# Attention and mixture-of-experts on one core: each pair's load of queries and keys issued four steps earlier on ScalarE's queue

## The chip, the cores and the metric

The kernel runs on one core of one Trainium2 chip. The metric is the device time of one execution in microseconds (us). Engines are named as in the profile: PE (TensorE), PEld (its weight loads), DVE (VectorE), ACT (ScalarE), POOL (GpSimd), SP (SyncE). A q behind a name (ACTq, SPq) is that engine's sequencer, which also issues its DMAs: an issue does not occupy the arithmetic of the engine, but it stands in the engine's program order, and a wait in front of it holds back whatever follows on that engine.

## The reference, cut to what matters

The input holds 8 batches of 8 heads with 576 positions and a head width of 64. Attention is thresholded: per query only the keys whose score is within tau of the row's maximum are kept. Its result, 4608 tokens of width 512, goes through a mixture of 8 experts, one expert per token.

```python
scores = scale * np.matmul(q, k.transpose(0, 1, 3, 2))
thresh = np.max(scores, axis=-1, keepdims=True) - tau
scores = np.where(scores >= thresh, scores, -1000000000.0)
attn = softmax(scores)
x = (attn @ v) as tokens [4608, 512]
expert_idx = argmax(x @ w_gate)
out[token] = gate * relu(x @ w1[expert]) @ w2[expert]
```

## The kernel before, in words

**Pairs and steps.** Two heads form a pair, so there are 32 pairs (n = 0 to 31), four to a batch. The order of the instructions of every engine is written out by hand: a loop (`one_step`, L1333) counts a step number k, each pair takes 10 steps, and what is planned for step k is issued in four slots of it (FRONT, BET, MID, END). Pair n's second set of scores, the exponentials, the masks and the casts stand in steps 10n to 10n+9; its first set of scores (for the maxima) stands 20 steps earlier. In the first, attention, part of the profile a step takes some 1.5 us (a pair took 14.84 us from 63.52 to 78.36 us).

**What a pair needs before its scores.** Every product is made in split precision, so queries and keys are brought in as 32-bit numbers and turned into a high and a low 16-bit part:

- `load_qk(n)`, L287: one DMA of 576 KB from HBM into a tile `qkf`; there are two `qkf` buffers, so the load of pair n writes over that of pair n-2. For n above 2 it is issued by ACT. Its step is given below.
- `split(n)`: an activation in place on ACT (L301, it scales), four steps later a cast to the high part on ACT (L303), one step after that the low part on POOL (L304). L304 is the last reader of `qkf`.
- `stack(n)` at step 10n-30: six copies on SP's queue (L319, L320, L321, after a small constant fill, L314) out of the tile `z` into the operands QK and ck, and two on ACT's queue into CQ (L325, three steps apart at the most).
- `row(p)`, L433: three DMAs of 2.2 KB on ACT's queue that put the row maxima of pair n (tile ptT) into CQ. The last of them stands three or four steps ahead of the pair's second scores, which read it.

```python
k = NSTEP * (n - 1) - LEAD - SL
if n >= 2:
    plan(max(first, k - LL), lambda n=n: load_qk(n))
if n > 1:
    plan(max(first + 1, k - TUNE["sp0"]) if n > 2 else first + 1, lambda n=n: split(n))
if n:
    plan(max(first + 3, k) if n > 1 else first + 2, lambda n=n: stack(n))
```

Here NSTEP, LEAD and SL are all 10, sp0 is 8 and first is -20. So k is 10n-30, the split stands at 10n-38, and the load at 10n-30-LL.

**The batch's transposing transfers.** When the last pair of a batch (n = 3, 7, 11, ...) has left PSUM, `finish(b)` plans for each of its four or five token blocks a transposing DMA on SP's queue (L629). For batches 0 to 5 they stand at steps 10n+37 to 10n+39, two to a step. With m = n+8 this is 10m-43 to 10m-41: they share their first step with the load of pair m as long as LL is 13. So six loads (m = 11, 15, 19, 23, 27, 31) stand beside such transfers.

**The rest.** SP also issues the load of the values (L291) and, later, those of the experts' weights. After attention the experts' products (h and y, L377) fill PE to the end.

Of the kernel before, what the change touches and what calls it, by code (L numbers as in the profile page):

```python
# [45 lines left out]
CAP = NTOK  # L46

TUNE = dict(
    lgp=6, rkp=6, hi=4, lo=5, rd=5, lead=10, r0=2, rs=1, r2=1, pl=0, pa=3, q0=1, qd=1, lgs=2, rks=2, c1=2, c3=1, c5=1, sl=10, ll=13, sp0=8, sps=0, lv=-9, sv=5, t0=16, av=2, tr=4, d=2, lg=5, d5=2, d6=2, d7=1, lg7=15, km=16, rate=15, dh=1, do=3, w1d=5, plv=1, xv=3, so=0, sto=0, ord=0, sc=5, fa=3, fd=4, wa1=-70, w2=38, wa2=-86, wl1=-28, wl2=-6, avb=2, route=1, ranks=7, pp=8, ew=4, maskat=0, w1a=-35, w0=19, w1b=3,
)  # L50


# [1409 lines left out]
```

## Time and profile before

| | us |
|---|---|
| median of 3 runs | 923.08 |
| lowest and highest run | 919.82, 925.15 |
| profiled execution, its own time | 923.2 |
| its span (first to last instruction) | 921.4 |
| PE busy | 887.7 (96% of the span) |
| DVE busy | 646.7 (70%) |
| ACT busy | 612.4 (66%) |
| POOL busy | 566.0 (61%) |

Shares are of the whole span and mix two stages: attention, up to about 490 us, where four engines work side by side, and the experts, where PE works nearly alone. A wait matters where PE idles; the view of waits by engine tells how often and for whom. DMA queues are named by number in the profile (q1 is that of SP, q10 that of ACT).

### The profile page before, as it was taken

Reading aid. Unit: us, or ns where it says so; the run is one execution under the profiler, and the core shown is the slowest. Engines: PE = TensorE matmul, PEld = TensorE weight load, DVE = VectorE, ACT = ScalarE, POOL = GpSimd, SP = SyncE. Lnnn points to the kernel's source line nnn. Section 1 sums busy time; section 2 is a strip of 40 time slices with the busy share of each in tenths; the row PEclk is TensorE's granted clock in tenths of the full one; section 3 lists DMA queues with packets and bytes.
Section 4 is the critical chain, followed back from the end, with each engine's and each line's share of the span. In section 5 each row is a group of like instructions: output and inputs, shape, how many; then the busy total and the mean of one; then the engine's idle time right before and its main releaser. Section 6 shows DMA issues by size and latency. Waiting matters only on the chain.

```text
span 921.4 us, 25091 instructions
## 1 busy us (share of the span) xinstructions
PE 887.7 (96%) x9983; PEld 643.0 (70%) x9983; DVE 646.7 (70%) x1322; ACT 612.4 (66%) x1040; POOL 566.0 (61%) x483
## 2 busy tenths in 40 slices
PE   4899999999999999999998999999999999999996
PEld 1377777777777677777776858666666666667773
DVE  7999898989898889898998856745333341524551
ACT  4789999999989889999889534444333351533561
POOL 7579887999999989989989733323222222222122
PEclk8999999999999999999999999999999999999998
DMA  8555484585774865956747695999565765547540
GB/s 200 136 124 132 111 172 119 154 188 137 194 164 133 155 143 164 190 138 175 142 130 147 215 191 193 292 306 344 165 201 159 178 174 164 180 147 225 183 173 27
DMA packets 173908, 158.14 MB, mean 172 GB/s; under 512 B 130201, under 2 KB 146075, under 8 KB 173788
## 3 DMA queue, kind: packets, MB, share of 16 engines
q1 hardware_dynamic: 152956, 105.38, 46.5%
q0 software_dynamic: 8992, 29.18, 9.5%
q10 hardware_dynamic: 11840, 21.94, 8.7%
q8 instruction: 80, 1.31, 0.6%
q14 instruction: 40, 0.33, 0.1%
HBM read 90.56 MB, written 19.17 MB: 119 GB/s over the span
## 4 chain that ended last, share of the span: by engine, by line
PE 78%; issue 6%; POOL 5%; DVE 4%; DMA 3%; ACT 2%; SPq 0%; ACTq 0%; POOLq 0%
PE h L377 19%; PE y L377 17%; PE st L447 7%; PE s L392 6%; PE s L396 6%; PE st L377 6%; PE av L536 4%; PE av L517 4%; PE av L542 3%; PE av L546 2%; PE av L547 2%; PE av L545 2%; POOL pl L484 2%; DVE nm L408 1%; DMA out_dram<-o,gt 1%
## 5 line engine op out<-in xcount | busy, mean ns | idle before, releaser
L484 POOL TENSOR_TENSOR pl<-e,ph 128x1024 f16<-128x1024 f32 x95 | 204.0, 2147 | 41.5 <-ACT ph L483 36.3
L408 DVE TENSOR_REDUCE nm<-s 128x1 f32<-128x512 f32 (+1 forms) x320 | 202.2, 637 | 14.7 <-PE s L396 9.9
L377 PE MATMUL y<-wb,hl 128*128 128x512 f16 (+2 forms) x1104 | 196.8, 347 | 1.7 <-issue 1.7
L377 PEld LDWEIGHTS <-wb 128*128 128x128 f16 x2304 | 183.1, 98 | 20.7 <-issue 2.8
L377 PE MATMUL h<-xTm,wb 128*128 128x256 f16 (+3 forms) x2112 | 190.1, 251 | 2.1 <-issue 2.1
L948 DVE SCALAR_TENSOR_TENSOR wb<-wf,wb 128x1024 f16<-128x1024 f32 x96 | 118.5, 1267 | 71.6 <-ACT wb L945 70.2
L377 PEld LDWEIGHTS <-hl 128*128 128x128 f16 (+2 forms) x1104 | 89.0, 98 | 100.0 <-issue 4.3
L392 PE MATMUL s<-QK 128*128 128x512 f16 (+3 forms) x640 | 138.0, 293 | 11.1 <-POOL QK L137 8.1
L1094 POOL DMA_INDIRECT out_dram<-o,gt x39 | 45.2, 1159 | 160.3 <-ACT o L1091 151.7
L396 PE MATMUL s<-ck,CQ 128*128 128x512 f16 (+3 forms) x640 | 142.5, 291 | 0.0
L447 PE MATMUL st<-QK 128*128 128x512 f16 (+3 forms) x640 | 135.7, 289 | 4.8 <-DVE e L478 2.9
L478 DVE SCALAR_TENSOR_TENSOR e<-st,e 128x512 f32<-128x512 f32 x192 | 129.5, 676 | 13.5 <-ACT e L475 11.9
L475 ACT ACTIVATE e<-st,ntau 128x512 f32<-128x512 f32 x192 | 131.0, 685 | 7.3 <-PE st L377 4.7
L945 ACT ACTIVATE wb<-wf 128x1024 f16<-128x1024 f32 x96 | 98.2, 1052 | 52.9 <-DMA wf<-in_w_dram 39.8
L377 PE MATMUL st<-CQ,ck 128*128 128x512 f16 (+3 forms) x640 | 130.7, 286 | 1.0 <-DMA CQ<-ptT 1.0
L459 ACT ACTIVATE e<-st,ntau_f 128x512 f32<-128x512 f32 (+1 forms) x160 | 93.6, 610 | 23.4 <-PE st L377 19.8
L517 PEld LDWEIGHTS av<-vf,e 128*128 128x128 f32 x512 | 91.6, 190 | 20.0
L483 ACT CAST ph<-e 128x1024 f16<-128x1024 f32 x96 | 99.6, 1037 | 5.9 <-issue 3.6
L1042 ACT ACTIVATE hl<-h 128x512 f16<-128x512 f32 (+2 forms) x78 | 43.9, 572 | 86.3 <-PE h L377 78.5
L546 PE MATMUL av<-vop,pl 128*128 128x65 f16 x768 | 96.5, 194 | 1.1 <-POOL pl L484 1.1
L545 PE MATMUL av<-vop,ph 128*128 128x64 f16 x768 | 96.6, 193 | 0.0
L547 PE MATMUL av<-vop,ph 128*128 128x65 f16 x768 | 95.6, 193 | 0.0
(227 smaller groups left out, 1547.6 us busy)
## 6 DMA issues: line engine op xcount, KB each, us to landing
wf<-in_w_dram SPq DMA_DIRECT2D x96, 512.0 KB
QK<-z SPq DMA_DIRECT2D x124, 144.0 KB
qkf<-in_qk_dram ACTq DMA_DIRECT2D x29, 576.0 KB
vf<-in_v_dram SPq DMA_DIRECT2D x31, 320.0 KB
ck<-z SPq DMA_DIRECT2D x62, 72.0 KB
CQ<-z ACTq DMA_DIRECT2D x58, 72.0 KB
x<-in_qk_dram SPq DMA_DIRECT2D x6, 288.0 KB
CQ<-ptT ACTq DMA_DIRECT2D x96, 2.2 KB
```

Source lines behind the costliest of these rows:

```text
L377: x = nc.tensor.matmul(*a, **kw).ins
L392: nc.tensor.matmul(sc[rows, oc], d["QA"][a][:, cols], d["KB"][a][:, CH[c]], start=True, stop=False)
L396: nc.tensor.matmul(sc[rows, oc], d["CQ"][:, at:at + cols.stop - cols.start], d["CK"][a][:, CH[c]], start=False, stop=True,)
L408: nc.vector.tensor_reduce(o, sc[:, 0:width(t)], axis=AX.X, op=ALU.max, negate=True)
L447: nc.tensor.matmul(sc[rows, oc], d["KB"][a][:, cols], d["QA"][a][:, CH[c]], start=True, stop=False)
L475: nc.scalar.activation(pf, sc, AF.Exp, bias=ntau, scale=0.125 / SS)
L478: masks.append(nc.vector.scalar_tensor_tensor(pf, sc, 0.0, pf, ALU.is_ge, ALU.mult).ins)
L484: (nc.vector if (n, t) in PLV else nc.gpsimd).tensor_tensor(l, pd, h, ALU.subtract)
L517: nc.tensor.matmul(av[:, a], d["Pf"][tv][:, q], vf[:, tv], start=False, stop=False)
L545: nc.tensor.matmul(av[rows, a, 0:D], h, vop[:, tv, W:W + D], start=False, stop=False)
L546: nc.tensor.matmul(av[rows, a], l, vop[:, tv, 0:W], start=False, stop=False)
L948: low = nc.vector.scalar_tensor_tensor(o[:, :, 1], x, SW, o[:, :, 0], ALU.mult, ALU.subtract)
```

## The change

One number of the table that sets the order is another: LL, by which the load stands ahead of `stack(n)`, is 17 in place of 13.

```diff
 TUNE = dict(
-    ..., sl=10, ll=13, sp0=8, ...
+    ..., sl=10, ll=17, sp0=8, ...
 )
```

The load of pair n moves from step 10n-43 to step 10n-47. Their number, size and source are the same. The load of pair 2, on SP's queue, keeps its place, since the earliest step bounds it; that of pair 3 moves past no other instruction and that of pair 4 past one cast; the 27 others, of pairs 5 to 31, move past some 13 rows of ACT each. Nothing is moved on PE, DVE, POOL and SP through the whole of attention.

ACT around the load of pair 23, before, at the place where the load will stand. L301 is the split of pair 22, L325 the second query copy of pair 21, L433 a row of maxima of pair 19, and L475 and L459 are exponentials of pair 18:

```order
L475 ACTIVATE e_2_5925<-st_2_5922,ntau 128x512
L425 ACTIVATE ptT_5920<-pst_5918,thr 9x128
L301 ACTIVATE qkf_5817<-qkf_5817 128x1152
L475 ACTIVATE e_2_5925<-st_3_5952,ntau 128x512
L325 DMA CQ_105<-z_5629 64x576
L459 ACTIVATE e_8_5982<-st_8_5977,ntau_f 128x512
L459 ACTIVATE e_10_5989<-st_10_5984,ntau_f 128x64
L427 CAST ptT_5920<-pst_5918 9x128
L433 DMA CQ_107<-ptT_5920 1x9x128
```

The same place of ACT in the changed kernel:

```order
L301 ACTIVATE qkf_5658<-qkf_5658 128x1152
L475 ACTIVATE e_2_5925<-st_3_5952,ntau 128x512
L325 DMA CQ_105<-z_5629 64x576
L287 DMA qkf_5962<-in_qk_dram 128x1152
L459 ACTIVATE e_8_5984<-st_8_5979,ntau_f 128x512
L459 ACTIVATE e_10_5991<-st_10_5986,ntau_f 128x64
L427 CAST ptT_5920<-pst_5918 9x128
L433 DMA CQ_107<-ptT_5920 1x9x128
L483 CAST ph_0_5878<-e_0_5877 128x1024
```

The load of pair 23 now stands between the query copy and the exponential L459, and ahead of all three rows of maxima (L433). Before, it stood behind the three rows:

```order
L475 ACTIVATE e_4_6079<-st_4_6076,ntau 128x512
L433 DMA CQ_107<-ptT_5920 1x9x128
L303 CAST z_5934<-qkf_5817 128x2x576
L475 ACTIVATE e_4_6079<-st_5_6104,ntau 128x512
L287 DMA qkf_6114<-in_qk_dram 128x1152
L598 CAST R_194<-xn_5872 128x4x128
```

The row L287 is gone from this place; the others stand there as before.

SP in the same steps reads alike in both kernels (here of the change): the last three copies of pair 21, a load of values, the five transposing transfers of batch 3, and then pair 22:

```order
L319 DMA QK_1_8416<-z_8154 64x2x576
L320 DMA QK_1_8416<-z_8154 64x1152
L321 DMA ck_1_99<-z_8154 64x576
L291 DMA vf_111<-in_v_dram 128x10x64
L629 DMA_TRANSPOSE xTg_0_8641<-R_195 128x8x128 x2
L629 DMA_TRANSPOSE xTg_2_8664<-R_195 128x8x128 x2
L629 DMA_TRANSPOSE xTg_4_8686<-Rh_196 128x8x128
L314 DMA CQ_106<-before 3x18x64
L319 DMA QK_0_8717<-z_8459 64x2x576
```

By program step the load stood beside the transposing transfers; it now stands beside the copies of pair 21, ahead of the transfers.

## Rows read from the trace of the kernel before

**Rows 1.** The page: the span, and PE's busy time.

```profile
span 921.4 us, 25091 instructions
PE 887.7 (96%) x9983; PEld 643.0 (70%) x9983; DVE 646.7 (70%) x1322; ACT 612.4 (66%) x1040; POOL 566.0 (61%) x483
```

**Rows 2.** Busy by stretch: PE, PEld, DVE, ACT, POOL, then clock, DMA share, GB/s.

```profile
50.00:485.00 435.00, 432.98 (x5834) 330.43 (x5833) 394.96 (x851) 392.67 (x719) 395.75 (x258) 1.00 0.65 151
```

**Rows 3.** Waits of PE, whole execution: total us, times, longest us.

```profile
PE st L447 <- DVE e L478: 2.9, 5, 1.5
...
PE s L392 <- DMA ck<-z: 1.6, 1, 1.6
```

**Rows 4.** Waits of all engines from 300 to 326 us.

```profile
DVE e L478 <- ACT e L475: 2.7, 2, 2.5
ACT qkf L301 <- DMA qkf<-in_qk_dram: 2.7, 1, 2.7
...
PE st L447 <- DVE e L478: 1.5, 1, 1.5
```

**Rows 5.** ACT in order of time, 300 to 326 us: start, us, line.

```profile
303.35 0.52 ACTq L325 DMA_DIRECT2D CQ<-z  x1
...
305.22 0.69 ACT L459 ACTIVATE e<-st,ntau_f 128x512 f32<-128x512 f32 x1 [0.30 <-PE st L377]
...
310.30 0.33 ACTq L287 DMA_DIRECT2D qkf<-in_qk_dram  x1
...
320.45 1.16 ACT L301 ACTIVATE qkf<-qkf 128x1152 f32<-128x1152 f32 x1 [2.73 <-DMA qkf<-in_qk_dram]
```

**Rows 6.** SP's queue in order of time, at two batches' transposing transfers.

```profile
122.62 9.57 SPq L629 DMA_TRANSPOSE xTg<-R  x4
...
308.19 12.00 SPq L629 DMA_TRANSPOSE xTg<-R  x4
```

**Rows 7.** As rows 2: around the load of pair 23, and around that of pair 8.

```profile
304.00:308.00 4.00, 4.00 (x86) 3.32 (x83) 3.99 (x11) 3.45 (x7) 3.98 (x4) 1.00 0.74 219
...
310.00:312.00 2.00, 2.00 (x21) 1.66 (x21) 1.57 (x3) 2.00 (x4) 2.00 (x2) 1.00 1.12 192
312.00:314.00 2.00, 2.00 (x25) 1.47 (x24) 1.92 (x4) 1.87 (x4) 1.84 (x3) 1.00 1.78 94
314.00:316.00 2.00, 2.00 (x19) 1.35 (x18) 1.99 (x5) 2.00 (x6) 2.00 (x2) 1.00 0.48 34
...
86.00:88.00 2.00, 2.00 (x21) 1.75 (x20) 1.92 (x4) 1.86 (x4) 2.00 (x2) 1.00 0.66 259
```

**Rows 8.** ACT in order of time, a pair without transposing transfers (load of pair 8).

```profile
76.52 0.54 ACTq L325 DMA_DIRECT2D CQ<-z  x1
78.10 0.69 ACT L459 ACTIVATE e<-st,ntau_f 128x512 f32<-128x512 f32 x1 [0.43 <-PE st L377]
...
83.48 0.72 ACTq L433 DMA_DIRECT2D CQ<-ptT  x1
84.30 0.42 ACTq L287 DMA_DIRECT2D qkf<-in_qk_dram  x1
...
90.80 1.15 ACT L301 ACTIVATE qkf<-qkf 128x1152 f32<-128x1152 f32 x1
```

**Rows 9.** The tile qkf, whole execution: engines' idle time that a load ended.

```profile
  DMA qkf<-in_qk_dram: 2.7, 1
```

**Rows 10.** SP and PE in order of time: pair 6's last copy, pair 4's and 6's first scores.

```profile
76.64 0.60 SPq L321 DMA_DIRECT2D ck<-z  x1
...
86.93 0.38 PE L447 MATMUL st<-QK 128*128 128x512 f16 x1
...
87.52 0.38 PE L392 MATMUL s<-QK 128*128 128x512 f16 x1
```

**Rows 11.** POOL and ACT in order of time, around the place of pair 16's load in the change.

```profile
195.24 2.38 POOL L304 TENSOR_TENSOR z<-qkf,z 128x1152 f16<-128x1152 f32 x1
...
196.67 0.51 ACTq L325 DMA_DIRECT2D CQ<-z  x1
...
198.25 0.69 ACT L459 ACTIVATE e<-st,ntau_f 128x512 f32<-128x512 f32 x1 [0.43 <-PE st L377]
```

More of the change, by code (lines that the diff above doesn't have):

```diff
@@ L48 @@
 TUNE = dict(
-    lgp=6, rkp=6, hi=4, lo=5, rd=5, lead=10, r0=2, rs=1, r2=1, pl=0, pa=3, q0=1, qd=1, lgs=2, rks=2, c1=2, c3=1, c5=1, sl=10, ll=13, sp0=8, sps=0, lv=-9, sv=5, t0=16, av=2, tr=4, d=2, lg=5, d5=2, d6=2, d7=1, lg7=15, km=16, rate=15, dh=1, do=3, w1d=5, plv=1, xv=3, so=0, sto=0, ord=0, sc=5, fa=3, fd=4, wa1=-70, w2=38, wa2=-86, wl1=-28, wl2=-6, avb=2, route=1, ranks=7, pp=8, ew=4, maskat=0, w1a=-35, w0=19, w1b=3,
+    lgp=6, rkp=6, hi=4, lo=5, rd=5, lead=10, r0=2, rs=1, r2=1, pl=0, pa=3, q0=1, qd=1, lgs=2, rks=2, c1=2, c3=1, c5=1, sl=10, ll=17, sp0=8, sps=0, lv=-9, sv=5, t0=16, av=2, tr=4, d=2, lg=5, d5=2, d6=2, d7=1, lg7=15, km=16, rate=15, dh=1, do=3, w1d=5, plv=1, xv=3, so=0, sto=0, ord=0, sc=5, fa=3, fd=4, wa1=-70, w2=38, wa2=-86, wl1=-28, wl2=-6, avb=2, route=1, ranks=7, pp=8, ew=4, maskat=0, w1a=-35, w0=19, w1b=3,
 )
```

## The prediction

> **What bounds the kernel now.** I read the page first, then the busy times of attention, then PE's waits, and only then the loads. The page shows PE busy for 887.7 of 921.4 us [rows 1], which alone would leave 33.7 us for any gain. The stretch that the change touches leaves far less: from 50 to 485 us PE is busy 432.98 of 435 us [rows 2], so in all of steady attention PE idles 2.0 us. DVE, ACT and POOL are busy about nine tenths of the same stretch. PE is the bound; a change in the loads can win back 2.0 us there at the most, and it can lose much more.
>
> Where are the 2.0 us? PE waits 2.9 us in all for the mask L478, five times, 1.5 us of it at once [rows 3]. The view of all waits shows that piece between 300 and 326 us with its chain: the split L301 of pair 23 waits 2.7 us for its load on ACT, the next exponential is late, the mask waits 2.5 us for it, and PE waits 1.5 us for the mask [rows 4]. So one late load explains three quarters of PE's idle time in attention. Over the whole execution it is the only load that ended a wait [rows 9].
>
> Why was it late? It was issued at 310.30 and its reader started at 320.45, having waited for it: 10.15 us [rows 5]. Pair 8's load, with no transposing transfers beside it, was issued at 84.30 and read at 90.80 without a wait [rows 8]; it had at most 6.5 us. Around pair 23 the SP queue was in its transposing transfers from 308.19 on, and four issues took 12.00 us, against 9.57 us for the four of batch 0 [rows 6]. The transfer rates show what went wrong: 192 GB/s with the transposing transfers alone, then 94 and 34 GB/s in the four microseconds in which the load's packets were beside them; a load by itself shows 259 GB/s [rows 7]. The two did not just share the engines: together they moved 256 KB in 4 us, where either alone moves over 750 KB. At 192 GB/s that takes 1.3 us, so about 2.7 us were lost, which is the split's wait.
>
> **The change, part by part.** *The six loads beside transposing transfers.* Pair 23's load will be issued right behind the query copy that ends at 303.87 [rows 5], which is 6.4 us earlier and 4.3 us before the first transposing issue at 308.19 [rows 6]. It then shares the engines with pair 21's copies, in a stretch that moved 219 GB/s at a DMA share of 0.74 [rows 7]. Its reader wants it no earlier than 320.45 - 2.73 = 317.7 [rows 5], so it has 13.8 us from issue in place of 7.4. Even a repeat of the 10.15 us would end the wait. Gain: the 1.5 us of PE [rows 4]. The five other such loads ended no wait, so they give nothing.
>
> *The other loads.* They had time enough and get more. Gain: 0.
>
> *The load's own issue, and its wait for POOL.* The load writes over the buffer of the pair two before, whose last reader is L304 on POOL, so its place on ACT must be behind that reader's end. In a common pair ACT's sequencer is free from the end of the query copy, 77.06, to the exponential at 78.10, which waits for PE in any case [rows 8]. The issue takes 0.42 us [rows 8], so 0.62 us is left for a wait. The worst place that I found is pair 16's: the reader ends at 195.24 + 2.38 = 197.62, the query copy at 197.18, so the load waits 0.44 us, and with the 0.42 us of issue it is through at 198.04, before the exponential at 198.25 [rows 11]. Cost: 0, covered by ACT's own wait for PE; without that cover the cost would be at most 0.86 us of ACT there.
>
> *What stands behind it on the queues.* SP's instructions don't move. Pair 6's last copy is issued at 76.64, and its first scores run at 87.52 [rows 10], so a delay of the copies by the load's time at full rate (about 590 KB at 259 GB/s, some 2.3 us) is within the 10.9 us. PE waited for such a copy once in the whole execution, 1.6 us [rows 3]. On ACT's queue the rows of maxima now follow the load. The last one is issued at 83.48 and PE needs it at 86.93 [rows 8, 10]; the load will have been issued 6.4 us ahead of it. Cost: 0 as long as the load lands within those 6.4 us, as pair 8's did.
>
> *The start.* The loads of pairs 3 and 4 move past one cast between them. Cost and gain: 0; bounds of 0.5 us either way, about one issue.
>
> *The sum.* 923.2 us, the profiled execution's own time, less 1.5 us: **921.7 us**. The median shown, 923.08, is 0.1 us lower, so the sum stands for it as well. The bounds of the gain are 0 (no such event in the median execution) and 2.0 us (all of PE's idle time there).
>
> **A rule to set against the trace.** The rows show a rate of 34 GB/s with both kinds of transfer outstanding [rows 7]. The Trainium skill, page "DMA: Bandwidth & Descriptors", section "Issuing engines are not separate DMA queues", says that transfers of all issuing engines end up on the same 16 DMA engines and interleave. By that rule alone, putting the load elsewhere only changes what it interleaves with, and nothing would be gained: 923.2 us, against 921.7 by the rows. The trace agrees that they share, but shows more than sharing: a fair share of 192 GB/s would not have fallen to 34.
>
> **The rivals.** *No change, 923.2 us.* The slow stretch might not come from this pairing but from something that strikes now and then, and strike at the new place. For it: of six loads beside transposing transfers five caused no wait [rows 9], and the four issues of batch 0 took 9.57 us, with no wait behind them [rows 6]. Against it: the 34 GB/s stand exactly where both were in flight, and the new place leaves 13.8 us. That is also the time by the section of the Trainium skill's page "DMA: Bandwidth & Descriptors" named above.
>
> *More is won, about 919.5 us.* The collision may strike a different number of batches in each execution; the three runs lie 5.3 us apart (919.82 to 925.15). If the median execution holds two or three strikes at 1.5 us, the change saves 3 to 4 us. For it: all six batches offer the chance. Against: the profiled execution, close to the median, holds one.
>
> *Slower: a row of maxima gets stuck behind the load, 933.7 us.* Load and rows are on the same queue. If a load beside copies and values, running into the transposing transfers, takes 10.15 us as the one of pair 23 did, it lands 10.15 us after its issue, while PE needs the row 86.93 - 77.06 = 9.9 us after that point [rows 8, 10], and the row's own way, up to 3.45 us, comes on top. PE then waits between 0.3 and 3.7 us; with 2 us in each of six batches it is 12 us. The point from which it decides is a load in flight for more than 6.4 us. Against it: the load starts 4.3 us before the transposing transfers.
>
> *Slower: ACT waits for POOL, 928.1 us.* If POOL ran later by one of its operations of 2.1 us against ACT, the load of pair 16 would wait 2.6 us in place of 0.44 and hold ACT 1.9 us beyond its cover. Pair 23 shows that 2.73 us of ACT cost 1.51 us of PE, so that is 1.07 us, six times (the loads beside or just behind a batch's end, where POOL is latest) 6.4 us. It decides from 0.62 us of wait on. Against it: POOL's order is the same as before, and ACT moves hardly at all.
>
> **How the numbers follow.** The forecast has 0.61, no change 0.18, more won 0.12, the stuck row 0.05, the wait for POOL 0.04. The range, **919.0 to 924.5 us**, takes in the first three with their bounds and about half of the scatter of the runs; what is left out is the slower pair and the tails, under 0.2. A difference of 0.5%, 4.6 us, is about what a measurement of this kernel can tell from no change. Faster by more needs three strikes saved: 0.05. Slower by more holds most of the last two rivals: 0.07. Within it: 0.88.
>
> **What would show it.** Right: in the profile after, no wait of L301 for its load; the piece of 1.5 us at PE gone, and PE idle for about 0.5 us from 50 to 485 us; loads in flight ahead of the transposing transfers, whose four issues no longer reach 12 us; no wait of ACT in front of L287 that delays L459. Wrong: PE waiting for CQ's rows (CQ<-ptT) once or more per batch, or new waits of L459 and of masks with the load's semaphore in front, or a late split in spite of the earlier issue. The whole is wrong if the time leaves the range although these signs are as I say.

## The result and the profile after

The changed kernel is slower: a median of 930.65 us (13 runs, 925.2 to 933.75) against 920.89 us for the kernel before (13 runs, 919.82 to 928.62). The ratio is 1.0072, with a 95% interval of 1.0051 to 1.0094: about 6.6 us (the medians lie 9.8 us apart), where 1.5 us of gain were forecast. The profiled execution took 932.4 us. Its page, to be read beside [rows 1]:

```profile
span 930.7 us, 25080 instructions
...
PE 892.7 (96%) x9983; PEld 644.3 (69%) x9983; DVE 645.7 (69%) x1322; ACT 610.9 (66%) x1040; POOL 563.2 (61%) x483
```

Busy by stretch (PE, PEld, DVE, ACT, POOL, clock, DMA share, GB/s), to be read beside [rows 2], and for a piece of 37 us:

```profile
50.00:485.00 435.00, 429.62 (x5776) 326.05 (x5775) 388.86 (x836) 386.61 (x712) 389.98 (x253) 1.00 0.64 150
...
180.00:217.00 37.00, 34.05 (x448) 24.88 (x447) 29.67 (x66) 29.47 (x59) 32.67 (x22) 1.00 0.67 156
...
485.00:560.00 75.00, 69.81 (x915) 53.94 (x914) 55.17 (x125) 47.17 (x89) 51.96 (x43) 0.95 0.73 170
```

In attention (50 to 485 us) PE idles for 5.38 us, where it idled for 2.02 us; 2.95 us of it lie between 180 and 217 us, where the kernel before has none. The last column but two is the clock that PE was granted; 0.95 behind attention stands for two stretches of 3.4 us at 1.2 GHz in place of 2.4, the first of them right after 1.4 us of idle PE at 511 us. The kernel of the eighth run below has such a stretch at 505 us and is not slower, so I lay no weight on it. The kernel before, from 180 to 217 us:

```profile
180.00:217.00 37.00, 37.00 (x534) 28.50 (x533) 34.15 (x76) 33.63 (x65) 34.67 (x23) 1.00 0.79 175
```

PE's waits from 50 to 485 us in the changed kernel, beside [rows 3]:

```profile
PE pst L420 <- DVE r L415: 1.9, 3, 0.6
PE st L447 <- DVE e L478: 1.2, 1, 1.2
PE st L447 <- DVE e L460: 0.8, 1, 0.8
PE st L377 <- DMA CQ<-ptT: 0.8, 1, 0.8
...
```

The forecast part did come: no split waits for its load in this profile. Pair 23's load goes out at 309.38, the transposing transfers behind it are through faster, and its split L301 has no wait in brackets (ACT, then SP, in order of time; beside [rows 5] and [rows 6]):

```profile
309.38 0.54 ACTq L287 DMA_DIRECT2D qkf<-in_qk_dram  x1
...
323.05 1.15 ACT L301 ACTIVATE qkf<-qkf 128x1152 f32<-128x1152 f32 x1
```

```profile
315.18 0.37 SPq L291 DMA_DIRECT2D vf<-in_v_dram  x1
316.07 6.45 SPq L629 DMA_TRANSPOSE xTg<-R  x4
322.57 2.01 SPq L629 DMA_TRANSPOSE xTg<-Rh  x1
```

Four issues took 6.45 us in place of 12.00. This holds beyond the two profiles: at this batch the four issues took 6.3 to 7.0 us in all seven profiles, of the runs below too, in which the load of pair 23 stands ahead of them, and 8.0 to 12.5 us in the nine in which it goes out beside them. But a split waited for its load in only three of the eight profiles with these loads at their old place (in one, the eighth kernel's, all but the last): in that of the kernel before and in two below, the eleventh and the fourteenth kernel's. The tile qkf there, whole execution, beside [rows 9]:

```profile
  DMA qkf<-in_qk_dram: 3.0, 1
...
  DMA qkf<-in_qk_dram: 2.2, 1
```

The second kernel, with every load at its old place, shows no such wait, and PE idle for only 0.39 us from 50 to 485 us. So the 1.5 us were there to be won in some executions only.

What is new stands around the load of pair 16, behind the five transposing transfers that SP issues while pair 12 is worked on. ACT in order of time, changed kernel:

```profile
197.78 0.52 ACTq L325 DMA_DIRECT2D CQ<-z  x1
...
198.94 0.33 ACTq L287 DMA_DIRECT2D qkf<-in_qk_dram  x1
199.36 0.89 ACT L459 ACTIVATE e<-st,ntau_f 128x512 f32<-128x512 f32 x2
200.14 0.24 ACT L427 CAST ptT<-pst 9x128 f16<-9x128 f32 x1
204.59 0.79 ACTq L433 DMA_DIRECT2D CQ<-ptT  x1
205.43 1.04 ACT L483 CAST ph<-e 128x1024 f16<-128x1024 f32 x1 [5.04 <-DMA xTg<-Rh]
...
206.86 0.77 ACTq L433 DMA_DIRECT2D CQ<-ptT  x1
...
207.95 0.72 ACTq L433 DMA_DIRECT2D CQ<-ptT  x1
```

The same rows of maxima in the kernel before:

```profile
198.38 0.79 ACTq L433 DMA_DIRECT2D CQ<-ptT  x1
...
200.61 0.77 ACTq L433 DMA_DIRECT2D CQ<-ptT  x1
...
204.71 0.72 ACTq L433 DMA_DIRECT2D CQ<-ptT  x1
205.53 0.42 ACTq L287 DMA_DIRECT2D qkf<-in_qk_dram  x1
```

Before, the first row of maxima went out at 198.38, right behind an exponential that waits for PE, and the load stood behind all three. Now ACT's sequencer stands in front of the first row for over 4 us, from the cast L427 (through at 200.38) until 204.59, and everything behind it stands too: the cast L483 shows 5.04 us of idle time, and the trace names the last transposing transfer (xTg<-Rh) as what ended it. SP had issued that transfer at 197.68, and it was itself late:

```profile
186.40 0.93 SPq L321 DMA_DIRECT2D ck<-z  x1
190.75 0.37 SPq L291 DMA_DIRECT2D vf<-in_v_dram  x1
191.55 6.08 SPq L629 DMA_TRANSPOSE xTg<-R  x4
197.68 1.65 SPq L629 DMA_TRANSPOSE xTg<-Rh  x1
```

A row of maxima uses nothing of that transfer. The link is in the program's rows with their waits. In this program the DMAs that SP and ACT issue turn over eight completion semaphores (DMAHW0 to 7; a semaphore counts landings, and an instruction can wait for a count) in one common order, and each waits until the one eight places ahead, on the same semaphore, has landed; so the DMAHW that a row waits for is also the one that it then holds itself. ACT's three rows of maxima in question (L433), and SP's last two transposing transfers and the three DMAs behind them, before:

```
L433 DMA CQ_104<-ptT_3697 1x9x128 [waits DMAHW7_49,Activation_49]
L433 DMA CQ_104<-ptT_3697 1x9x128 [waits DMAHW2_49,Activation_49]
L433 DMA CQ_104<-ptT_3697 1x9x128 [waits DMAHW5_49,DVE_49]
L629 DMA_TRANSPOSE xTg_2_3614<-R_195 128x8x128 [waits DMAHW7_49]
L629 DMA_TRANSPOSE xTg_4_3636<-Rh_196 128x8x128 [waits DMAHW0_49]
L314 DMA CQ_106<-before 3x18x64 [waits DMAHW2_49,PE_49]
L319 DMA QK_0_3667<-z_3409 64x2x576 [waits DMAHW3_49,Activation_49]
L320 DMA QK_0_3667<-z_3409 64x1152 [waits DMAHW5_49,Pool_49]
```

and after, where the load stands ahead of the rows and counts as one place:

```
L287 DMA qkf_3739<-in_qk_dram 128x1152 [waits DMAHW6_49,Pool_49]
L433 DMA CQ_104<-ptT_3697 1x9x128 [waits DMAHW0_49,Activation_49]
L433 DMA CQ_104<-ptT_3697 1x9x128 [waits DMAHW3_49,Activation_49]
L433 DMA CQ_104<-ptT_3697 1x9x128 [waits DMAHW6_49,DVE_49]
L629 DMA_TRANSPOSE xTg_4_3636<-Rh_196 128x8x128 [waits DMAHW0_49]
L319 DMA QK_0_3667<-z_3409 64x2x576 [waits DMAHW3_49,Activation_49]
```

So the first row now waits for the last transposing transfer in place of the one before it, the second for the first copy of the next pair, the third for the load itself. In the same way the values' load L291 on SP comes to wait for pair 15's load, which was issued at 183.35 (both on DMAHW3): it goes out 3.4 us after the copy ahead of it is through, at 190.75, and the transposing transfers follow.

What this costs: by the first scores of each pair, PE runs 0.9 us later than before up to pair 13, 5.4 us later at pair 17 (4.5 us lost at this one place), 4.0 us at pair 22 (the event of pair 23's load is gone, 1.4 us back), and 6.5 us later at pair 31. Pairs 13 and 17, before and then after:

```profile
192.83 0.38 PE L392 MATMUL s<-QK 128*128 128x512 f16 x1
253.53 0.38 PE L392 MATMUL s<-QK 128*128 128x512 f16 x1
...
193.74 0.38 PE L392 MATMUL s<-QK 128*128 128x512 f16 x1
258.98 0.38 PE L392 MATMUL s<-QK 128*128 128x512 f16 x1
```

The idle time of 2.95 us is the smaller measure of the same loss, since the ends of matmuls are modelled in the profile. The rest of the 9.3 us between the two spans comes after attention and differs from one execution to the next (2.4 and 1.1 us in two profiles of one program, the fourth and eleventh below).

### The profile page after: what moved, and what is told of

It reads as the page before. It is cut to its first block, busy times and chain, and to the rows that moved or that the text cites. A ratio compares the mean times of both kernels' runs of the same rounds, so it can differ in the third digit from the quotient of the medians.

```text
span 930.7 us, 25080 instructions
## 1 busy us (share of the span) xinstructions
PE 892.7 (96%) x9983; PEld 644.3 (69%) x9983; DVE 645.7 (69%) x1322; ACT 610.9 (66%) x1040; POOL 563.2 (61%) x483
## 5 line engine op out<-in xcount | busy, mean ns | idle before, releaser
L475 ACT ACTIVATE e<-st,ntau 128x512 f32<-128x512 f32 x192 | 131.1, 685 | 8.2 <-PE st L377 7.2
L483 ACT CAST ph<-e 128x1024 f16<-128x1024 f32 x96 | 99.7, 1039 | 14.7 <-DMA xTg<-Rh 9.7
L459 ACT ACTIVATE e<-st,ntau_f 128x512 f32<-128x512 f32 (+1 forms) x160 | 93.1, 611 | 23.8 <-PE st L377 19.3
L460 DVE SCALAR_TENSOR_TENSOR e<-st,e 128x512 f32<-128x512 f32 (+1 forms) x160 | 91.2, 585 | 12.7 <-ACT e L459 10.8
```

The lines of the kernel that those rows point to most:

```text
L475: nc.scalar.activation(pf, sc, AF.Exp, bias=ntau, scale=0.125 / SS)
L483: nc.scalar.copy(h, pd)
```

## The experiments

Theory A: the sharing of semaphores as such makes the row late. Theory B: the load merely crowds the DMA engines where it now stands, a little for each load. Every diff below that moves loads changes this one line of the kernel before, and LL is 13 there unless it is said otherwise.

**1 and 2: the sharing without the load's move, and the reverse.** A 128-byte DMA on SP, ahead of the first copy of pairs 14, 22 and 30, shifts the turn of the semaphores by one. In the changed kernel it takes the first row off the last transposing transfer; in the kernel before it puts it there.

```diff
+            if n in (14, 22, 30) and i == 0:
+                nc.sync.dma_start(pads, before[96:97, 0:64])
```

> Edit: the changed kernel with one DMA of 128 bytes more on SP's queue, behind each batch of five transposing transfers (three in all), so that the first row of maxima behind it no longer shares its completion semaphore with the last transposing transfer. Theory A (shared semaphores: every eighth DMA of SP and ACT together has the same one and waits for the one before): the three waits of 4.4, 1.5 and 2.0 us on ACT go and with them 5 to 7 of the 9.8 us lost: 923 to 926 us. Theory B (the load at its new place only crowds the copies and the transposing transfers on the DMA engines): the time stays at 929 to 932 us.

> Edit: the same three small DMAs put into the kernel before, where they do the opposite: the first row of maxima now comes to share its semaphore with the last of five transposing transfers, with every load at its old place. Theory A: ACT waits for that landing three times, but the transposing transfers start as early as before, so each wait is short, 0 to 1.5 us, and the time 921 to 924 us; the trace must show this wait by name. Theory B: 921 us, no wait of a row of maxima.

The first took 929.75 us (4 runs; 1.0098, interval 1.0064 to 1.0133), the second 922.39 us (10 runs; 1.0004, 0.9980 to 1.0027); the kernel before took 922.91 us beside them. The first lies where theory B put it, not A. Sharing alone costs nothing that can be told (as far as the first row goes; over the whole second execution one cast stands for 1.9 us behind such a row, at 443 us), so theory A as I had put it fell. But the first is no proof that it plays no part: the wait had only gone over to the second row and its partner, a first copy of the next pair. ACT's longest wait from 180 to 217 us there (numbers of lines are 3 higher in this kernel):

```profile
ACT vop L349 <- DMA QK<-z: 4.1, 1, 4.1
```

**3 and 4: half of the loads each.** Only those of pairs 7, 11, 15 ... (beside the transposing transfers before the change), and only those of pairs 5, 6, 9, 10 ...

```diff
-            plan(max(first, k - LL), lambda n=n: load_qk(n))
+            plan(max(first, k - (17 if n % 4 == 3 else 13)), lambda n=n: load_qk(n))
```
```diff
+            plan(max(first, k - (17 if n % 4 in (1, 2) else 13)), lambda n=n: load_qk(n))
```

> Edit: only the loads of pairs 3, 7, 11, ... (the six later ones stand beside transposing transfers) are issued four steps earlier, the others stay. The order of semaphores then puts a value load or a transposing transfer behind the load, and the row of maxima behind the last of five transposing transfers. Theory A: SP waits for the load's landing, the transposing transfers start 3 to 5 us later, and the row waits for the last of them: most of the loss, 925 to 930 us. Theory B: the loss goes by the number of moved loads, 7 of 28: about 923 us.

> Edit: only the loads of pairs with n mod 4 equal to 1 or 2 are issued four steps earlier; those beside and right behind the transposing transfers stay. Theory A: no row of maxima shares with the last of five transposing transfers and no value load or transposing transfer stands behind a load: no loss, 920 to 922 us. Theory B: half of the loads moved, half of the loss: 925 to 926 us.

They took 924.6 us (10 runs; 1.0027, 1.0005 to 1.0050) and 926.5 us (10 runs; 1.0046, 1.0022 to 1.0070), the first between what A and B said (925 to 930 and 923 us), the second far from A (920 to 922) and just above B (925 to 926). In the first, SP's values' load waits for a load as in the changed kernel (3.4 us at 189.72) and the transposing transfers are late, yet PE idles for only 1.06 us from 50 to 485 us. Late transfers alone are not enough. This left theory C: the loads of pairs 8, 12, 16 ..., which go out beside the last transposing transfer, slow it, and the row waits. Theory D is B as a plain sum, theory E puts the loss behind 485 us.

**5 to 8: with and without these loads, and by place.**

```diff
+            plan(max(first, k - (17 if n % 4 in (0, 3) else 13)), lambda n=n: load_qk(n))
...
+            plan(max(first, k - (17 if n % 4 else 13)), lambda n=n: load_qk(n))
...
+            plan(max(first, k - (17 if n < 28 else 13)), lambda n=n: load_qk(n))
...
+            plan(max(first, k - (17 if n >= 28 else 13)), lambda n=n: load_qk(n))
```

> Only the loads of every fourth pair's both neighbours move up: those of pairs 7, 11, 15 ... (whose landing the first transposing transfers or the values' load wait for) and those of pairs 8, 12, 16 ... (which then go out beside the last transposing transfer). Theory C (two loads in a chain: the first makes SyncE's queue about 3 us late, the second slows the last transposing transfer, and the row of maxima that shares its semaphore waits for it): the row behind the batch of pair 12 waits 4 to 5 us on ScalarE's queue at about 205 us, TensorE stands 2 to 3 us near 207 to 216, and the kernel takes 927 to 930 us, most of the loss with half of the moved loads. Theory D (a sum: each moved load costs about the same by crowding on the DMA engines): the loss is the 2.4 us of the first kind plus 1 us of the second, 926 us, and no wait of the row over 2 us.

> As the changed kernel, but the loads of pairs 8, 12, 16, 20 ... stay where they were, so that none goes out beside the last transposing transfer. Theory C: SyncE still waits 3 us for the load that shares a semaphore and the transposing transfers still start late, but the last of them lands within 4 us, the row waits 2 us at most, TensorE's idle time from 50 to 485 us is under 3 us (5.3 in the changed kernel), and the kernel takes 924 to 926.5 us. Theory D: only 8 of 32 loads moved back, about 929 us.

> As the changed kernel, but the loads of pairs 28 to 31 stay where they were. Theory C: the row's waits behind the batches of pairs 12 and 20 remain, 927 to 930 us. Theory E (the last moved loads disturb the passage from attention to the experts after 485 us, where two stretches at half clock and later matmuls stand in the changed kernel's profile): the loss after 485 us goes, 925 to 927 us.

> Only the loads of pairs 28 to 31 move up. Theory C and theory D: 922 to 924 us, no difference from the kernel before that can be told. Theory E: 925 to 927 us, with half-clock stretches between 495 and 545 us.

| kernel | median us (11 runs each) | ratio, 95% interval | PE idle 50 to 485 us |
|---|---|---|---|
| 5, pairs 4n and 4n+3 | 927.62 | 1.0071, 1.0041 to 1.0101 | 2.88 |
| 6, all but pairs 4n | 923.18 | 1.0017, 0.9988 to 1.0045 | 2.14 |
| 7, all but pairs 28 to 31 | 927.31 | 1.0059, 1.0022 to 1.0095 | 6.06 |
| 8, pairs 28 to 31 | 923.4 | 1.0014, 0.9987 to 1.0042 | 0.43 |

(Kernel before beside them: 921.36 us.) By time, C holds in the fifth, seventh and eighth; the sixth is 0.8 us quicker than C said (924 to 926.5), and D is out there (929 expected). E is out in the eighth; the seventh alone, 0.3 us above E's range, does not decide it. One more thing misses. In the fifth the row behind the batch of pair 12 waited 2.2 us, not 4 to 5, and PE idled 0.9 us from 180 to 217 us, not 2 to 3. And it was open whether the late transposing transfers are needed as well.

**9 to 11: which link is needed.** Ninth: only the loads of pairs 4, 8, 12 ..., so that SP's transposing transfers start on time. Tenth: the changed kernel with the loads of pairs 7, 11, 15 ... issued by GpSimd, whose transfers use other semaphores in this program, so that nothing on SP waits for them. Eleventh: the fourth kernel again.

```diff
+            plan(max(first, k - (17 if n % 4 == 0 else 13)), lambda n=n: load_qk(n))
```
```diff
-        (nc.scalar if n > 2 else nc.sync).dma_start(qkf, qk[n])
+        (nc.gpsimd if n % 8 in (3, 7) and n > 3 else nc.scalar if n > 2 else nc.sync).dma_start(qkf, qk[n])
```

> Only the loads of pairs 4, 8, 12, 16 ... move up, the ones that go out beside the last transposing transfer; the row of maxima shares its semaphore with that transfer, but no load shares one with the values' load or the first transposing transfer, so SyncE's queue is on time. Theory C with both links needed: the transposing transfers start at their old times, the last lands before the row's turn, the row waits 2 us at most, and the kernel takes 921 to 924 us. Theory C with the second link alone enough: the row waits 4 us or more at 200 to 206 us and the kernel takes 926 to 929 us. Theory D: about 1 us more than before, 922.5 us.

> As the changed kernel, but the loads of pairs 7, 11, 15 ... are issued by GpSimd, whose transfers turn over other semaphores: the loads go out at about the same time, and nothing on SyncE's queue waits for their landing any more; the loads beside the last transposing transfer stay moved. Theory C with both links needed: the transposing transfers start 3 us sooner, the row waits 2 us at most, TensorE stands idle for under 3 us from 50 to 485 us, and the kernel takes 922 to 926 us, if GpSimd's own work is not made late by issuing. Theory D: the same bytes at the same time, 929 to 931 us.

> The kernel that moves only the loads of pairs 5, 6, 9, 10 ... once more, since its first measurement (1.0046) stood against theory C and its profile shows no wait of a row. Theory C: the first measurement was partly chance, 922 to 924.5 us. Theory D: 925 to 927 us again.

The ninth took 926.62 us (6 runs; 1.0064, 1.0039 to 1.0088), the time that C with the second link alone gave. Its profile does not part the links cleanly: the transposing transfers start on time, at 188.14, but with pair 15's load beside them the four issues took 10.12 us, and the last transfer goes out as late as in the changed kernel, at 198.31. The waits are shorter than expected, two in a row. ACT in order of time:

```profile
199.44 0.37 ACTq L287 DMA_DIRECT2D qkf<-in_qk_dram  x1
...
202.78 0.79 ACTq L433 DMA_DIRECT2D CQ<-ptT  x1
203.61 1.04 ACT L483 CAST ph<-e 128x1024 f16<-128x1024 f32 x1 [2.56 <-DMA xTg<-Rh]
...
205.83 0.77 ACTq L433 DMA_DIRECT2D CQ<-ptT  x1
206.65 0.53 ACT L346 ACTIVATE vop<-vf 128x384 f16<-128x384 f32 x1 [1.41 <-DMA QK<-z]
```

The tenth took 928.73 us (10 runs; 1.0091, 1.0061 to 1.0121), but its edit did not do what it was meant to. GpSimd comes to the load only after its own work, so from pair 15 on the load goes out 0.3 to 1.2 us behind the first transposing transfer, beside it, as in the kernel before, and not 6.6 to 8.1 us ahead of it, as in the changed kernel. At pair 15 (POOL, then SP):

```profile
188.39 0.60 POOL L287 DMA_DIRECT2D qkf<-in_qk_dram  x1
...
187.69 11.28 SPq L629 DMA_TRANSPOSE xTg<-R  x4
199.01 1.35 SPq L629 DMA_TRANSPOSE xTg<-Rh  x1
```

The transposing transfers started on time, but the last is later than in the changed kernel, and the row waits for it (ACT idles 2.7 us). So this run says nothing about the first link. In its profile PE waits above all for rows of maxima that landed late, and from 50 to 485 us its waits for these are

```profile
PE st L377 <- DMA CQ<-ptT: 8.8, 6, 3.7
```

The eleventh took 924.59 us (12 runs; 1.0042, 1.0020 to 1.0064): the fourth kernel's 0.4% is real, and C does not explain it. (The median is just beyond the end of C's range, but the kernel before was at 920.65 us in these runs, so it is the ratio that compares.) In this profile a split waits 3.0 us for its load near 200 us, as in [rows 4], for the load of pair 15 is not moved here, and PE waits three times for rows that land late, 3.0 us in all. In the fourth kernel's profile no split waits, and PE waits for such a row once, 0.7 us; one program shows both pictures.

**12 to 14: two loads of 32.** Behind a batch of five transposing transfers only the loads of pairs 16 and 24 are left.

```diff
+            plan(max(first, k - (17 if n in (16, 24) else 13)), lambda n=n: load_qk(n))
...
+            plan(max(first, k - (13 if n in (16, 24) else 17)), lambda n=n: load_qk(n))
...
+            plan(max(first, k - (15 if n in (16, 24) else 13)), lambda n=n: load_qk(n))
```

> Only 2 of the 32 loads move up by four steps, those of pairs 16 and 24, which then go out on ScalarE's queue in front of the three rows of maxima that stand behind a batch of five transposing transfers, while the last of these and the next pair's first copies are on their way. Theory C, now with this link alone: the rows wait 1.5 to 4 us for the semaphores of those slowed transfers, TensorE's order slips by 2 to 4 us between pairs 13 and 17, and the kernel takes 925 to 928 us. Theory D: two loads of 32 cost next to nothing, 921 to 922 us.

> The changed kernel, but the loads of pairs 16 and 24 stay where they were. Theory C: most of the loss goes, 922 to 925 us, no wait of a row over 2 us behind the batches of pairs 12 and 20. Theory D: 930 us as in the changed kernel.

> The loads of pairs 16 and 24 move up by two steps in place of four: they go out between the second and the third row of maxima, 3 us or so later than in the changed kernel, when the last transposing transfer has landed. Theory C: the first two rows wait no longer than before; only the third follows the load; 920 to 924 us.

Beside a kernel before of 919.19 us (18 runs), the twelfth took 925.92 us (6 runs; 1.0081, 1.0049 to 1.0113), the thirteenth 925.06 us (7 runs; 1.0052, 1.0020 to 1.0085), the fourteenth 922.36 us (12 runs; 1.0032, 1.0002 to 1.0062). By time, two loads alone cost as much as the whole change. The chain is there in the profile, though smaller than forecast: PE loses 1.6 us between pairs 13 and 17 (2 to 4 were expected) and 0.7 us behind the batch of pair 20. This execution, 924.76 us, is a quick one of the six; where the rest of the 6.7 us between the medians is lost is not shown. ACT, twelfth kernel, in order of time:

```profile
198.37 0.33 ACTq L287 DMA_DIRECT2D qkf<-in_qk_dram  x1
...
199.40 0.79 ACTq L433 DMA_DIRECT2D CQ<-ptT  x1
...
204.00 0.77 ACTq L433 DMA_DIRECT2D CQ<-ptT  x1
204.81 0.53 ACT L346 ACTIVATE vop<-vf 128x384 f16<-128x384 f32 x1 [2.89 <-DMA QK<-z]
```

and SP, where nothing is late:

```profile
195.91 1.57 SPq L629 DMA_TRANSPOSE xTg<-Rh  x1
197.58 0.82 SPq L314 DMA_DIRECT2D CQ<-before  x1
198.51 0.67 SPq L319 DMA_DIRECT2D QK<-z  x1
```

The second row holds the semaphore of the copy that SP issued at 198.51, 0.14 us behind the load; the row goes out at 204.00, so that copy of 144 KB took until then, 5.5 us. In the thirteenth, without the load, the last transposing transfer is issued at 197.41 and the row that waits for it goes out at 200.87, 3.5 us later, against 6.9 us (197.68 to 204.59) in the changed kernel, whose program shares alike there (4.5 to 4.9 us in the fifth, seventh, ninth and tenth kernels, which have the load there too):

```profile
200.87 0.79 ACTq L433 DMA_DIRECT2D CQ<-ptT  x1
201.70 1.05 ACT L483 CAST ph<-e 128x1024 f16<-128x1024 f32 x1 [2.07 <-DMA xTg<-Rh]
```

With two steps in place of four, 1.0032 in place of 1.0081 (the intervals overlap): the first two rows go out ahead of the load, but the third follows it and lands late, and PE waits for it, 1.2 us near 209 us and 2.0 us between 305 and 342 us. The thirteenth lies above what C said (922 to 925 us): the other moved loads cost something too, 0.2 to 0.85%, though not on top of the two, since the changed kernel loses no more than the two alone. No kernel tried is faster than the one before.

## Why the prediction was wrong

*What bounds the kernel:* right. PE is the bound.

*What was to be won, 1.5 us off the sum:* right for the profiled execution, and there it was luck to catch one: a split waits in three of the eight profiles with these loads at their old place, in none of the seven with them moved (the tenth kernel left out). So as far as these profiles show, the move ends the collision, but the median execution need not hold one. The rival "no change" had this half right (something that strikes now and then); that it strikes at the new place was not seen. That the loss worked out from the rates, 2.7 us, equals the split's wait hangs on the stretch chosen: the sum took 312 to 316 us, and the transfers went on beside each other from 316 to 320 us, at 157 and 141 GB/s.

*The six loads beside transposing transfers:* right as to the load, which now has its bytes in before the transfers start (at pairs 15 and 23); not counted was what waits for its landing. "SP's instructions don't move" held for their order only: SP's values' load came to wait 3.4 us for pair 15's load. The third run shows that this by itself costs little, 1.0027.

*"The other loads. They had time enough and get more. Gain: 0."* **This is the step that failed.** I asked what the moved loads gain and not beside what they come to stand. The first transposing transfer stands at step 10m-43, pair m+1's load now at 10m-37, six steps or some 9 us later (8.3 us in the changed kernel's batch of pair 20, 316.07 to 324.40). Four issues took up to 12.00 us [rows 6], and a fifth follows in every second batch. So the move took pair 23's load out of the transfers' beginning and put pair 24's into their end, as it did for pair 16. In place of 0 us PE lost 4.5 us at pair 16's load, and the kernel that moves these two loads alone takes 1.0081. The rows to see this were there; I had compared step numbers with the program's neighbours and not with the transfers' duration.

*"What stands behind it on the queues ... Cost: 0 as long as the load lands within those 6.4 us":* wrong in the same way. I priced the row by when PE needs its data, in an ordinary pair [rows 8, 10]. The first row did not come late because the load was ahead of it in the queue, but because its issue waited for a semaphore that a slowed transfer held, and that wait stopped the whole of ACT, not only the row. The rival "a row of maxima gets stuck behind the load" (933.7 us, 0.05) had the right victim but the wrong chain, and six places where there are two; the forecast's exchange of ACT's delay for PE's (2.73 to 1.51 us) was near: here 4.2 us of ACT, from L427's end at 200.38 to 204.59, stand against 2.95 us of idle PE. Rows that land late, so that PE waits for them as that rival had it, do stand in the tenth, eleventh and fourteenth profiles; in the changed kernel PE waits for one once, 0.8 us.

*ACT's wait for POOL in front of the load:* right, at most 0.25 us at pairs 16 and 24.

*The start:* PE is 0.8 to 0.9 us late from pair 3 on, more than the 0.5 us given; but the second kernel, with its loads as before, is 0.8 us early there, so this much differs between executions.

*The rule weighed:* the Trainium skill, page "DMA: Bandwidth & Descriptors", section "Issuing engines are not separate DMA queues", says that transfers from all issuing engines share the 16 DMA engines and interleave. I set it aside for the rows' 34 GB/s. What followed from it, that the load only changes what it interleaves with, agrees with the trace: 3.5 us for the last transposing transfer without the load beside it and 6.9 us with it. That the loss would then be nothing did not follow.

*The number:* 921.7 us forecast, 919.0 to 924.5, measured 930.65; slower had 0.07. Of the other rivals, no change and more won did not come; they too counted only the event of pair 23.

*What stays open:* why the moves of the other loads cost 0.2 to 0.85% in the thirteenth and 0.4% in the fourth and eleventh kernels (PE's late rows of maxima are seen there in some executions, not their cause), how the 6.7 us of the twelfth kernel add up, and whether the load beside the slowed transfers would be harmless if no row shared a semaphore with them. So the chain from the load through the semaphore to ACT and PE is read from the traces; that the sharing is needed for the loss is not shown. The first run was meant to show that and only changed the partner; a kernel in which all three rows share with nothing of SP's was not tried.

## What to carry to other kernels

A transfer that is moved away from a collision lands somewhere: list what is in flight there, by the durations in the trace and not by steps, for each of the loads that move and not only for the one that was late. Look at the program's waits for DMA semaphores before and after: one more DMA ahead of another shifts every later pairing by one, and an issue then waits for a transfer that it has nothing to do with, with its whole engine. And two loads of 32 can cost as much as all of them: moving classes of loads told this, where the busy shares did not. An edit that is to hold a transfer's time and change its issuer has to be looked up in the trace: in the tenth kernel the new issuer came to it 5 us later.

## What the runs showed of the hardware

With a 576 KB load issued 0.8 to 1.5 us behind it, the last transposing transfer took 4.5 to 6.9 us from issue to the release of the next holder of its semaphore (ninth kernel to changed kernel), against 3.5 us without (thirteenth); a 144 KB copy issued 0.14 us behind such a load took 5.5 us (twelfth). An issue that waits for a semaphore held back what followed it for 4.2 us on ACT and for 3.4 us on SP (changed kernel). Sharing as such, with nothing slow on the other side, cost nothing that can be told (second kernel: 1.0004, 0.9980 to 1.0027). Four transposing issues took 6.3 to 7.0 us with the load of pair 23 ahead of them and 8.0 to 12.5 us with it beside them.
